# Reordering weight combinations and rebuilding the last drain in a Fourier-filter and SiLU-layer kernel

## The chip, the core and the metric

The kernel runs on one core of a Trainium2 chip. The metric is the device time of one execution in microseconds. The engines are called by the names of the profile: PE (TensorE), PEld (TensorE's weight loads), DVE (VectorE), ACT (ScalarE), POOL (GpSimd) and SP (SyncE, which here only issues DMAs). A name with a q, such as SPq, is the queue in which that engine issues DMAs or waits.

## What is computed

A Fourier filter over the sequence, then a two-matrix layer with a SiLU between. The weights come as 64-bit floats, everything else as 32-bit floats.

```python
X = np.fft.rfft(x, axis=1)                       # x: (8, 3008, 256)
Y = X * (filt_r + 1j * filt_i)[None, :, :]
y = np.fft.irfft(Y, n=x.shape[1], axis=1)
h = y.reshape(24064, 256) @ w_in                 # w_in: (256, 2048), 64-bit
g = h * (1.0 / (1.0 + np.exp(-h)))
out = g @ w_out                                  # w_out: (2048, 256), 64-bit
```

## The kernel before

The filter of each of the 8 sequences is done with small matrix multiplications in four stages (pa or pf, pb, pc, pd in the profile, with intermediate results written to DRAM and read back), and leaves the sequence in an SBUF tile y. The layer works on pieces of 256 or 240 tokens of two half-sequences at once, called pairs: 6 pairs a sequence, 48 in all. For each pair the 2048 inner columns are taken in 8 blocks of 256; one block of one pair is a step, so there are 384 steps, and one more in which only the last projection is left. Both matrix products use a Strassen-Winograd scheme, seven block products in place of eight. For that the weights need, beside their four blocks A11, A12, S3 and A22, three combinations, and S3 itself is replaced: `combine_weights` (line 853) computes in its part 0 S1 = S3 + A22 and S2 = S1 - A11, and in its part 1 S3 = A11 - S3 and S4 = A12 - S2.

A step has 8 rounds. In them `hidden(step)` (line 639) issues the seven products with the first matrix into the PSUM tiles px and pyz, their evictions and sums (abc and g) on ACT and DVE, and the SiLUs on ACT; `project(step - 1)` (line 698) issues the seven products of the step before with the second matrix into four PSUM accumulators acc. The two are interleaved round by round, so that one step's matmuls cover the other's work on DVE and ACT. The tiles px and pyz have one buffer each: TensorE can start the next product into one of them only when what was there has been read. In what follows, S4, S3, A11 and so on also name the matmul that uses this block; g0, g1 and g2 are the sums that `hidden` writes to g[:, 0], g[:, 1] and g[:, 2] (lines 663, 682 and 674).

Everything else is a list of pieces with a step and a round each: `put(step, round, piece)` (line 559), and similar entries for tokens and stores at the end of the program. The list is sorted by time, and after each round the pieces that are due are issued behind that round's work (`until`, line 1023). The order of the program on each engine is exactly this order; no scheduler changes it, and each engine works through its instructions in order.

Of these pieces the following matter here:

- The weights are rounded from 64 to 32 bits on the chip, 128 inner columns at a time (index j, 0 to 15; block jp = j // 2 of the weights needs both of its j). Weights 0 to 8 are done before the main loop. Weights 9 to 15 come in steps 0 to 6: `split` in round 1 (lines 812 to 816, on DVE and ACT), `rounded` (lines 828 to 834, on DVE), `placed` in round 5 (line 843, two DVE operations that write w_t). When j is odd the block is complete, and its combinations follow: part 0 in round 5 of the same step, part 1 in round 5 of the next one, and for j = 15 in the same one (lines 1001 to 1003). A combination is one DVE operation of 128 x 256, at line 623, the line of the helper `combine`.
- `tokens(pair)` (line 629) prepares three combinations of a pair's tokens on DVE; for pair 1 in step 7, round 1 (line 1015).
- Steps 0 to 7 also hold the first filter stage of the second sequence (`stage1`, line 325: two matmuls pa, two evictions on ACT, and DMAs by POOL at line 349).
- `drain(pair, i)` (line 719) is called when accumulator i of a pair is complete, in the order 0 to 3. It copies the accumulators to an SBUF tile s, alternately on ACT and DVE (lines 729 and 731), and then makes seven sums in s: on POOL, and for the last pair on DVE.
- `output(pair, chunk)` (line 736) transposes two of the four results of a pair (line 741) and issues eight stores of 28 or 32 KB (line 749), all by SP, and for the last pair by SP and ACT in turn. Chunk 0 needs outputs 2 and 6 of s, chunk 1 outputs 4 and 1.

Of the kernel before, what the change touches and what calls it, by code (L numbers as in the profile page):

```python
# [49 lines left out]
ALU = mybir.AluOpType  # L50
# [117 lines left out]
def kernel(  # L168
# [9 lines left out]
    nc = tc.nc  # L178
# [380 lines left out]
    def put(step, rnd, piece, *args):  # L559

        pending.append((step + rnd / ROUNDS, len(pending), lambda: piece(*args)))
# [55 lines left out]
    pairs = [(b, half, c0, n) for b in range(B) for half in range(2) for c0, n in PAIRS]  # L617
    n_steps = len(pairs) * NJP
    v, gp = nc.vector, nc.gpsimd
    ty, g_t, acc, unfinished = {}, {}, {}, []  # L620

    def combine(eng, out, in0, in1, op):
        eng.tensor_tensor(out=out, in0=in0, in1=in1, op=op)  # L623
# [5 lines left out]
    def tokens(pair):  # L629

        n, yt = pairs[pair][3], channels(pair)
        t = typool.tile([128, 4, CH], FP32, name=f"ty_{pair}", tag="ty")
        combine(v, t[:, 0:2, 0:n], yt[:, :, n:2 * n],
                yt[:, 0, 0:2 * n].rearrange("p (a n) -> p a n", a=2), ALU.subtract)
        combine(v, t[:, 2, 0:n], yt[:, 1, n:2 * n], t[:, 0, 0:n], ALU.subtract)
        combine(v, t[:, 3, 0:n], yt[:, 1, 0:n], t[:, 2, 0:n], ALU.subtract)
        ty[pair] = t
# [60 lines left out]
    def project(step):  # L698

        pair, jp = divmod(step, NJP)  # L700
        n, g = pairs[pair][3], g_t.pop(step)
        if jp == 0:
            acc[pair] = {}
        last = jp == NJP - 1

        order = PROJECT[2:3] + PROJECT[0:2] + PROJECT[3:] if jp == 0 else PROJECT
        for c, k, i, h in order:
            if i not in acc[pair]:
                acc[pair][i] = accps.tile([128, 2, 256], FP32, name=f"acc_{pair}_{i}", tag=f"a{i}")

            nc.tensor.matmul(out=acc[pair][i][:, h, 0:n], lhsT=w_t[:, jp, c, 1], rhs=g[:, k, 0:n],  # L711
                             start=(jp == 0 and h == 0), stop=last, skip_group_check=True)
            if last and (h == 1 or i == 3):
                drain(pair, i)
            yield
# [3 lines left out]
    def drain(pair, i):  # L719
        n = pairs[pair][3]  # L720

        if i == 0:
            results[pair] = spool.tile([128, 8, CH], FP32, name=f"s_{pair}", tag="s")
            if n < CH:
                gp.memset(results[pair][:, :, n:CH], 0.0)
        s = results[pair]
        copy = v.tensor_copy if i % 2 else nc.scalar.copy
        if i < 3:
            copy(out=s[:, 2 * i:2 * i + 2, 0:n], in_=acc[pair][i][:, :, 0:n])  # L729
            return  # L730
        copy(out=s[:, 6, 0:n], in_=acc.pop(pair)[3][:, 0, 0:n])
        eng = v if pair == len(pairs) - 1 else gp
        for o, a, b in ((2, 0, 2), (5, 0, 5), (3, 5, 3), (6, 3, 6), (0, 5, 1), (4, 0, 4), (1, 3, 1)):
            combine(eng, s[:, o, 0:n], s[:, a, 0:n], s[:, b, 0:n], ALU.add)

    def output(pair, chunk):

        b, half, c0, n = pairs[pair]
        o = opool.tile([128, 8, 2, 32], FP32, name=f"o_{pair}_{chunk}", tag="o")
        for h in range(2):  # L740
            v.transpose(out=o[:, :, h, :], in_=results[pair][:, ((2, 6), (4, 1))[chunk][h], :])
        row = (c0 + n * chunk) // 16
        for rr in range(2):
            cnt = (n // 16 - rr + 1) // 2
            t0 = b * S + 32 * (row + rr) + 16 * half
            for q in range(4):
                p0 = 32 * q + 16 * rr
                queue = nc.scalar if pair == len(pairs) - 1 and q % 2 else nc.sync
                queue.dma_start(
                    out=bass.AP(tensor=out.tensor, offset=out.offset + t0 * C + 64 * q,  # L750
                                ap=[[C, 16], [64 * C, cnt], [1, 64]]),
                    in_=o[p0:p0 + 16, 0:cnt].rearrange("p k h c -> p k (h c)"))
# [118 lines left out]
    def split(*js):  # L871
        if wide:
            split_weights(*js)

    def rounded(*js):
        if wide:
            round_weights(*js)
# [120 lines left out]
    for j in range(9, NJ):  # L998
        put(j - 9, 1, lambda j=j: (split(j), rounded(j)))
        put(j - 9, 5, placed, j)  # L1000
        if j % 2:
            put(j - 9, 5, combine_weights, j // 2, 0)
            put(j - 8 if j < 15 else j - 9, 5, combine_weights, j // 2, 1)

        if j < 11:
            put(j - 9, 1, weights, j + 5)

    per = len(PAIRS) * 2


    combines = ((-2, 1), (6, 1), (11, 5), (22, 5), (26, 6), (38, 1))
    stores = (((10, 1), (10, 5)), ((19, 1), (23, 5)), ((31, 1), (31, 5)), ((35, 1), (35, 5)),
              ((43, 1), (43, 5)), ((50, 1), (51, 1)))
    for pair in range(len(pairs)):
        step, rnd = combines[pair % per] if pair != 1 else (7, 1)
        pending.append((pair // per * STEPS + step + rnd / ROUNDS, 98, lambda pair=pair: tokens(pair)))
        for chunk in range(2):
            step, rnd = stores[pair % per][chunk]
            pending.append((pair // per * STEPS + step + rnd / ROUNDS, 99 + chunk,
                            lambda pair=pair, chunk=chunk: output(pair, chunk)))  # L1020
# [49 lines left out]
```

## Time and profile before

| | us |
|---|---|
| median of 4 runs | 2599.91 |
| lowest and highest of them | 2596.86, 2602.36 |
| the profiled execution, its own time | 2600.09 |
| its span in the trace | 2598.3 |
| PE busy in the span | 2566.3 |
| DVE busy | 1695.1 |
| ACT busy | 1105.4 |
| POOL busy | 423.9 |

The span runs from the first to the last event in the trace; the execution's own time has 1.8 us around it. The granted TensorE clock is 0.995 over the span. In the trace one matmul of the program stands as two, so "x2" in a line of PE is one product. A line of the timeline gives start, duration, engine, source line, operation, what is written and read, the number of instructions that were merged, and in brackets the idle time before it with the event that ended it. A merged line's duration runs from the start of its first instruction to the end of its last.

The first matmul of the main loop starts at 83.56 us; the last accumulation matmul ends at about 2587.5.

### The profile page before, as it was taken

What the parts mean: (1) busy time and instruction counts of PE and PEld (TensorE: products, weight loads), DVE (VectorE), ACT (ScalarE), POOL (GpSimd) and SP (SyncE); (2) the same over time, 40 slices, a digit from 0 to 9 for tenths busy, and PEclk for the clock granted to TensorE, in tenths of its full rate; (3) what the DMA queues carried; (4) which work ended last, traced back from release to release, by engine and by line L of the source; (5) the groups of instructions that cost most, each with busy time, mean ns of one, the idle gap of its engine ahead of it and who ended that gap; (6) DMA issues with size and microseconds to landing.
All of it is one profiled execution on the core that took longest, in us unless ns stands there. A gap on an engine that the chain in (4) does not pass through costs nothing.

```text
span 2598.3 us, 48343 instructions
## 1 busy us (share of the span) xinstructions
PE 2566.3 (99%) x18928; PEld 2186.9 (84%) x18928; DVE 1695.1 (65%) x3574; ACT 1105.4 (43%) x3015; POOL 423.9 (16%) x667
## 2 busy tenths in 40 slices
PE   8899999999999999999999999999999999999998
PEld 6688888888888888888888888888888888888987
DVE  7766666666666766666666676666666676555554
ACT  3544444444444444443444444444444444444443
POOL 2111211121112111311122111211121112101100
PEclk9899999999999999999999999999999999999999
DMA  8531232212222222222223222331223211201000
GB/s 273 143 89 45 68 78 65 66 56 79 62 57 66 76 65 56 62 78 67 62 64 77 62 66 57 73 81 50 63 71 75 72 41 26 60 18 21 9 17 16
DMA packets 200253, 171.08 MB, mean 66 GB/s; under 512 B 122324, under 2 KB 174388, under 8 KB 199236
## 3 DMA queue, kind: packets, MB, share of 16 engines
q1 hardware_dynamic: 178616, 117.07, 18.6%
q0 software_dynamic: 16864, 44.59, 5.5%
q10 hardware_dynamic: 4544, 6.33, 0.8%
q8 instruction: 149, 2.44, 0.4%
q14 instruction: 80, 0.66, 0.1%
HBM read 96.05 MB, written 81.26 MB: 68 GB/s over the span
## 4 chain that ended last, share of the span: by engine, by line
PE 97%; DMA 2%; DVE 1%; ACT 0%; ACTq 0%; issue 0%; SPq 0%; DVEq 0%
PE acc L711 44%; PE px L652 26%; PE pyz L652 19%; PE pd L538 3%; PE pb L433 2%; PE pc L469 2%; PE pf L403 1%; PE pa L331 0%; PE pa L340 0%; DMA filt<-in_filt_i_dram 0%; PE pc L491 0%; DMA w_t<-in_x_dram 0%; DMA t<-d 0%; DMA raw<-in_moe_w_in_dram 0%; DMA filt<-in_filt_r_dram 0%
## 5 line engine op out<-in xcount | busy, mean ns | idle before, releaser
L711 PE MATMUL acc<-g,w_t 128*128 128x256 f32 (+1 forms) x5376 | 1512.1, 375 | 0.4 <-DVE g L623 0.4
L711 PEld LDWEIGHTS acc<-g,w_t 128*128 128x128 f32 x5376 | 1021.4, 190 | 115.6 <-DVE g L623 0.8
L623 DVE TENSOR_TENSOR g<-pyz,abc 128x256 f32<-128x256 f32 (+1 forms) x1152 | 479.6, 416 | 538.1 <-ACT abc L673 297.2
L623 DVE TENSOR_TENSOR g<-g 128x256 f32<-128x256 f32 (+3 forms) x1152 | 616.8, 535 | 196.7 <-ACT g L656 183.5
L652 PE MATMUL px<-ty,w_t 128*128 128x256 f32 (+1 forms) x2304 | 686.8, 380 | 0.5 <-ACT abc L673 0.5
L656 ACT ACTIVATE g<-g 128x256 f32<-128x256 f32 (+1 forms) x1152 | 472.9, 411 | 245.8 <-DVE g L623 245.8
L623 POOL TENSOR_TENSOR s<-s 128x256 f32<-128x256 f32 (+1 forms) x329 | 259.8, 807 | 1454.4 <-DVE s L729 1438.1
L652 PEld LDWEIGHTS px<-ty,w_t 128*128 128x128 f32 x2304 | 424.0, 190 | 82.9 <-issue 25.9
L652 PE MATMUL pyz<-y,w_t 128*128 128x256 f32 (+1 forms) x1536 | 453.7, 377 | 0.7 <-DVE g L623 0.6
L652 PEld LDWEIGHTS pyz<-y,w_t 128*128 128x128 f32 x1536 | 283.4, 189 | 46.6 <-DVE g L623 5.8
L667 ACT COPY abc<-px 128x256 f32<-128x256 f32 (+1 forms) x384 | 141.3, 368 | 364.9 <-PE px L652 364.9
L656 ACT ACTIVATE g<-px 128x256 f32<-128x256 f32 (+1 forms) x384 | 145.8, 380 | 307.5 <-PE px L652 307.5
L673 ACT COPY abc<-px 128x256 f32<-128x256 f32 (+1 forms) x384 | 143.8, 374 | 309.9 <-PE px L652 309.9
L652 PE MATMUL px<-y,w_t 128*128 128x256 f32 (+1 forms) x768 | 229.6, 381 | 0.9 <-ACT y L246 0.9
L652 PE MATMUL pyz<-ty,w_t 128*128 128x256 f32 (+1 forms) x768 | 225.6, 375 | 0.0
L652 PEld LDWEIGHTS px<-y,w_t 128*128 128x128 f32 x768 | 141.9, 189 | 39.9 <-ACT g L656 15.4
L652 PEld LDWEIGHTS pyz<-ty,w_t 128*128 128x128 f32 x768 | 146.0, 190 | 16.9 <-DVE g L623 0.5
L660 ACT COPY abc<-px 128x256 f32<-128x256 f32 (+1 forms) x384 | 134.9, 351 | 2.5 <-PE px L652 1.1
L244 DVE COPY y<-pd 128x376 f32<-128x376 f32 x62 | 50.0, 806 | 102.1 <-PE pd L538 102.0
L538 PEld LDWEIGHTS pd<-wi_t,t 48*64 48x64 f32 x4096 | 67.5, 138 | 28.9 <-issue 28.9
L246 ACT COPY y<-pd 128x376 f32<-128x376 f32 x62 | 50.2, 809 | 87.2 <-PE pd L538 87.0
L538 PE MATMUL pd<-wi_t,t 48*64 48x47 f32 x4096 | 75.2, 237 | 9.3 <-DMA t<-d 9.0
(98 smaller groups left out, 1323.3 us busy)
## 6 DMA issues: line engine op xcount, KB each, us to landing
t<-d SPq DMA_DIRECT2D x120, 192.0 KB
d<-q POOLq DMA_DIRECT2D x86, 256.0 KB, 2.7
t<-d SPq DMA_DIRECT2D x84, 256.0 KB
out_dram<-o SPq DMA_DIRECT2D x636, 32.0 KB
d<-tf POOLq DMA_DIRECT2D x144, 96.0 KB, 2.4
xr<-in_x_dram SPq DMA_DIRECT2D x6, 1472.0 KB
x_all<-in_x_dram SPq DMA_DIRECT2D x72, 96.0 KB
x_all<-xr SPq DMA_DIRECT2D x72, 96.0 KB
```

What stands on the lines that cost most here:

```text
L244: nc.vector.tensor_copy(out=dst, in_=src)
L246: nc.scalar.copy(out=dst, in_=src)
L433: nc.tensor.matmul(out=ps[k][32 * j:32 * j + 32, ri, :], lhsT=d_t[rows, 4 * g + at, ri, :], rhs=t2[rows, at, :], start=True, stop=True)
L469: nc.tensor.matmul(out=ps[j][64 * k:64 * k + 64, a, :], lhsT=e_t[rows, g + a, k, ri, :], rhs=zs[k][rows, ri, :], start=(a == 0 and ri == 0 ...
L538: nc.tensor.matmul(out=ps[h][c0:c0 + 64, cb, i, :], lhsT=t4s[g][rows, i, 128 * cb + c0:128 * cb + c0 + 64], rhs=wi_t[rows, :], start=True, ...
L623: eng.tensor_tensor(out=out, in0=in0, in1=in1, op=op)
L652: nc.tensor.matmul(out=out, lhsT=w_t[:, jp, c, 0], rhs=rhs, start=start, stop=True, skip_group_check=True)
L656: nc.scalar.activation(out=g[:, k, 0:n], in_=g[:, k, 0:n] if src is None else src, func=AFT.Silu)
L660: nc.scalar.copy(out=sums[:, 0, 0:n], in_=xo)
L667: nc.scalar.copy(out=sums[:, 1, 0:n], in_=xo)
L673: nc.scalar.copy(out=sums[:, 2, 0:n], in_=xo)
L711: nc.tensor.matmul(out=acc[pair][i][:, h, 0:n], lhsT=w_t[:, jp, c, 1], rhs=g[:, k, 0:n], start=(jp == 0 and h == 0), stop=last, skip_group ...
```

## The change

There are three parts. First, the combinations of weights 9, 11, 13 and 15 move: part 0 from the step of the rounding to the next one (for 15 to round 6 of the same step), and part 1 one step further than part 0 (for 13 to step 6, round 1; for 15 to step 7, round 1). In the order of DVE this puts part 0 of 9, 11 and 13 ahead of line 843's operations of weights 10, 12 and 14, part 1 of 9 and 11 ahead of those of weights 11 and 13, part 1 of 13 ahead of the split of weight 15, and takes two of the four combinations behind weight 15's placement to the next step. Pair 1's tokens go from round 1 to round 5 of step 7.

Second, the last pair's drain doesn't copy all accumulators: a new function copies the first one and half of the third on ACT, and the sums take the other operands straight from PSUM, on DVE. Outputs 2 and 6 are computed first, chunk 0 is transposed and its stores are issued, and only then follow the three sums of chunk 1. Two copies on DVE fall away; the number of sums stays seven.

Third, the last pair's stores: chunk 0's eight are issued by SP (three), ACT (three) and POOL (two), chunk 1's by SP and ACT (four each).

The instructions of PE and their order stay as they are.

```diff
@@ drain
         s = results[pair]
+        if pair == len(pairs) - 1:
+            return drain_last(pair, i, n, s, acc[pair])
         copy = v.tensor_copy if i % 2 else nc.scalar.copy
...
-        eng = v if pair == len(pairs) - 1 else gp
         for o, a, b in ((2, 0, 2), (5, 0, 5), (3, 5, 3), (6, 3, 6), (0, 5, 1), (4, 0, 4), (1, 3, 1)):
-            combine(eng, s[:, o, 0:n], s[:, a, 0:n], s[:, b, 0:n], ALU.add)
+            combine(gp, s[:, o, 0:n], s[:, a, 0:n], s[:, b, 0:n], ALU.add)
+
+    def drain_last(pair, i, n, s, sums):
+
+        def add(o, a, b):
+            combine(v, s[:, o, 0:n], s[:, a, 0:n], b, ALU.add)
+        if i == 0:
+            nc.scalar.copy(out=s[:, 0:2, 0:n], in_=sums[0][:, :, 0:n])
+        elif i == 1:
+            add(2, 0, sums[1][:, 0, 0:n])
+        elif i == 2:
+            add(5, 0, sums[2][:, 1, 0:n])
+            nc.scalar.copy(out=s[:, 4, 0:n], in_=sums[2][:, 0, 0:n])
+            add(3, 5, sums[1][:, 1, 0:n])
+        else:
+            add(6, 3, sums[3][:, 0, 0:n])
+            output(pair, 0)
+            for o, a, b in ((0, 5, 1), (4, 0, 4), (1, 3, 1)):
+                add(o, a, s[:, b, 0:n])
+            output(pair, 1)
@@ output
-                queue = nc.scalar if pair == len(pairs) - 1 and q % 2 else nc.sync
+                queue = nc.sync
+                if pair == len(pairs) - 1:
+                    turn = (0, 1, rr, 2) if chunk == 0 else (0, 1, 0, 1)
+                    queue = (nc.sync, nc.scalar, nc.gpsimd)[turn[q]]
@@ for j in range(9, NJ)
         if j % 2:
-            put(j - 9, 5, combine_weights, j // 2, 0)
-            put(j - 8 if j < 15 else j - 9, 5, combine_weights, j // 2, 1)
+
+            put(*((j - 8, 5) if j < 15 else (j - 9, 6)), combine_weights, j // 2, 0)
+            put(*((j - 7, 5) if j < 13 else (j - 7 if j == 13 else j - 8, 1)), combine_weights, j // 2, 1)
@@ for pair in range(len(pairs))
-        step, rnd = combines[pair % per] if pair != 1 else (7, 1)
+        step, rnd = combines[pair % per] if pair != 1 else (7, 5)
...
-        for chunk in range(2):
+        for chunk in range(2 if pair < len(pairs) - 1 else 0):
```

## Prediction

> **What bounds the kernel now.** I read the page first, then two stretches that the diff touches: the first eight steps of the main loop and the end.
>
> ```profile
> span 2598.3 us, 48343 instructions
> PE 2566.3 (99%) x18928; PEld 2186.9 (84%) x18928; DVE 1695.1 (65%) x3574; ACT 1105.4 (43%) x3015; POOL 423.9 (16%) x667
> PE 97%; DMA 2%; DVE 1%; ACT 0%; ACTq 0%; issue 0%; SPq 0%; DVEq 0%
> ```
>
> TensorE is busy in 99% of the span and is 97% of the chain that ended last. No matmul is added or removed, so only its idle time can be won: 2598.3 - 2566.3 = 32 us, most of it before the main loop, which the diff doesn't touch. The stretch table (us, length, then busy time and instructions of PE, PEld, DVE, ACT, POOL, clock, DMA share, GB/s), cut at the first matmul of each step, gives what lies in steps 1, 2, 6, 7 and 8:
>
> ```profile
> 91.10:99.43 8.33, 8.26 (x34) 6.01 (x34) 6.72 (x17) 4.65 (x12) 2.23 (x5) 1.00 0.47 145
> 99.43:107.28 7.85, 7.85 (x33) 5.93 (x32) 6.24 (x16) 4.41 (x12) 1.97 (x5) 1.00 0.71 210
> ...
> 131.33:139.18 7.85, 7.85 (x34) 5.94 (x33) 6.24 (x16) 4.42 (x12) 1.97 (x5) 1.00 0.69 164
> 139.18:147.83 8.65, 8.03 (x34) 5.99 (x33) 5.22 (x13) 3.50 (x10) 2.04 (x6) 1.00 0.19 46
> 147.83:153.87 6.04, 6.04 (x29) 5.29 (x28) 3.46 (x8) 3.34 (x10) 0.79 (x2) 1.00 0.65 178
> ```
>
> Step 8 is pure matmul work: 6.04 us. Steps 1 to 7 also have two stage-1 matmuls, 1.72 us in the chain, so their work is 7.76. They take 8.33, 7.85, 8.10, 7.85, 8.10, 7.85, 8.65 (steps 3 to 5 are in the same table): 2.41 us over the work. In the timeline (start, us, engine, line, operation, [idle before it and its releaser]) the end of step 0 and of step 6:
>
> ```profile
> 90.25 0.75 DVE L843 TENSOR_TENSOR w_t<-m,e 128x256 f32<-128x256 f32 x2
> 91.03 0.88 DVE L623 TENSOR_TENSOR w_t<-w_t 128x256 f32<-128x256 f32 x2
> 91.84 0.42 DVE L623 TENSOR_TENSOR g<-pyz,abc 128x256 f32<-128x256 f32 x1
> ...
> 138.88 1.55 DVE L623 TENSOR_TENSOR w_t<-w_t 128x256 f32<-128x256 f32 x4
> 140.35 0.41 DVE L623 TENSOR_TENSOR g<-pyz,abc 128x256 f32<-128x256 f32 x1
> 140.82 0.70 PE L652 MATMUL pyz<-y,w_t 128*128 128x256 f32 x2 [0.62 <-DVE g L623]
> ```
>
> VectorE places rounded weights (L843), combines them (w_t<-w_t), and only then reads pyz (g<-pyz); TensorE's next step waits for that read. At the end:
>
> ```profile
> 2585.61 1.89 PE L711 MATMUL acc<-g,w_t 128*128 128x240 f32 x8 [0.41 <-DVE g L623]
> 2586.37 0.56 ACT L729 COPY s<-acc 128x480 f32<-128x480 f32 x1 [1.51 <-PE acc L711]
> ...
> 2587.86 2.68 DVE L623 TENSOR_TENSOR s<-s 128x240 f32<-128x240 f32 x7
> 2590.46 1.42 DVE L741 STREAM_TRANSPOSE o<-s 128x256 f32<-128x256 f32 x4
> 2591.25 3.77 SPq L749 DMA_DIRECT2D out_dram<-o  x8
> 2591.25 3.97 ACTq L749 DMA_DIRECT2D out_dram<-o  x8
> ```
>
> After TensorE's last matmul (2587.5): 3.7 us of copies, seven sums and two transposes until the first store, 4.0 us of issuing, then about 3.1 us of landing and closing.
>
> [...] The trace has 402 for s<-s. [...] the trace has 0.41 us for g<-pyz at 240 beside 0.40 for s<-s, so I take nothing[...]. [...] here issuing (0.36 to 0.49 us a store) sets the pace. [...] POOL's four issues from 97.99 take 1.97 us (498 ns each) beside VectorE's w_t work.
>
> **Weights, part by part.** VectorE, ScalarE and TensorE form a loop through each step: g1 (g<-pyz) -> silu -> three g operations -> split L812 -> ScalarE L814, L816, L667, silu, two evictions, L673 -> g2 -> weight work -> g1. Its length sets steps 1 to 6. By the starts of g1 it is 7.85 us in odd steps (91.84 to 99.69; weight work: part-1 combinations, two independent operations, ahead of L843, 98.35 to 99.69 = 1.34), and 8.10 in even ones (99.69 to 107.79; L843, then part-0 combinations that need it and each other, 106.20 to 107.79 = 1.59). So: independent order 0.67 + 0.67; waiting for L843 0.11 more; the dependent pair 0.14 more.
> - Step 0: part 0 leaves. g1 is then held by its matmul (S4 ends about 91.15): 91.18 instead of 91.84, gain 0.66. In step 1 the stage-1 matmuls come only 0.34 earlier, since TensorE won only that; the second eviction waits for them, and L673 comes 0.52 earlier. Gain 0.52.
> - Steps 1, 3, 5: part 0 ahead of L843 instead of part 1: +0.14 each. Steps 2, 4: part 1 ahead of L843 instead of part 0 behind it: -0.25 each. Gain after step 5: 0.52 - 0.42 + 0.50 = 0.60.
> - Step 6: part 1 of weight 13 goes into round 1, ahead of split(15). Behind it on VectorE stand L812 and L815, and ScalarE's L814, L816, then L667 wait for those: +0.67, so TensorE stalls again at S3 and A22. Part 1 of weight 15 leaves the end of the step: -0.66. Net nothing: g1 about 139.75 instead of 140.35, TensorE's pyz 140.22 instead of 140.82.
> - Step 7: part 1 of weight 15 (0.67) takes the tokens' place in round 1; TensorE reads S3 only at about 144. Tokens (1.5 us) move to round 5, between g2 and g1: g1 about 147.57, where its matmul alone would give 147.43. Cost 0 to 0.14. Nothing needs the tokens before step 8, round 2. From step 8 VectorE has 2.6 us free a step.
> Sum: **-0.55 us** (bounds: -0.1 if step 6 and 7 cost their full price at TensorE; -3.1 if all 2.41 and step 0's 0.66 went).
>
> **The end, part by part.** The first copy on ScalarE ends 2586.93. Pitches from the seven s<-s: 0.42 for an add that needs the one before, 0.33 otherwise (3 x 0.42 + 3 x 0.33 = 2.25 from first to last start; measured 2.26).
> - Sums of outputs 2, 5, 3, 6 from 2586.96: starts 2586.96, 2587.29, 2587.71, 2588.13. The last accumulator is ready at 2587.51, so no add waits for TensorE. VectorE's two copies (0.66 + 0.41) go. [...]
> - Four semaphore checks, 0.1 us apart, stand ahead of each chunk's first transpose (2589.83 to 2590.12 in the trace of before, under two adds). Behind one add they show about 0.1. Transposes 2588.58, 2588.94; chunk 0 stores from **2589.35** (before 2591.25).
> - Three adds 2589.27, 2589.69, 2590.02, transposes to 2591.10: chunk 1 ready 2591.12.
> - Chunk 0 has three stores on SP, three on ACT, two on POOL; the HW queues issue theirs by 2590.8. Chunk 1: four each from 2591.12, last starts about 2592.45 (SP) and 2592.5 (ACT), against 2594.58 and 2594.78. A store also waits until the earlier store with its semaphore has landed: before, chunk 1 started at 2593.21 and 2593.45, 1.96 and 2.20 after those of chunk 0. Now the first of chunk 1 take free ones and the second ones come 2.1 to 2.2 after theirs: at most 0.1.
> - POOL: two stores of 0.50 to 0.54 us (L349, L517), issued by 2590.45, landing 2.4 to 2.9 later (medians of the DMA table): 2593.4. ACT's last lands about 2592.5 + 2.2 = 2594.7. Covered by 1.3 us. Nothing is queued behind POOL's two stores or ScalarE's waiting copy but ACT's own stores, which wait for VectorE anyway.
> - Packets: 2176 in 4.3 us before, at best 240 in 0.35 us, so 3.2 us at that rate; the new stretch is about 4 us.
> Sum: 2594.78 - 2592.55 = **-2.2 us** (bounds [...] -2.4 without the 0.1s).
>
> Total -2.75: 2600.09 (the profiled execution, span 2598.3 and 1.8 around it) becomes 2597.3. The median of the four is 2599.91, so **2597.2**.
>
> **Rivals.**
> 1. Weights give nothing: step 6's delay is not paid back because ScalarE's chain ends last there. For it: L667 and L673 are the releasers in the chain of step 6. Only the end: -2.2, 2597.7.
> 2. The end is bound by landing: 16 stores from three queues share the 16 DMA engines, which were 0.6 to 0.8 busy. If landing rises from 2.2 to 2.9, chunk 1's stores wait for chunk 0's: last at 2590.3 + 2.9 = 2593.2, -1.5; total -2.05, 2597.9.
> 3. More than the sum: all idle time of steps 0 to 7 goes, -3.1 and -2.4: 2594.4. Against it: the loop of 7.85 is longer than the work.
> 4. Slower: POOL's queue ends last. Its landings reached 18.3 us (L517) and 6.7 (L349) at most, beside other traffic. It decides from 2594.7 on; the kernel is slower once the second store lands over 2597.4, 7.5 us after its issue at 2589.9. At 18.3 it lands 2608.2, 10.7 us later: 2610. Against it: the queues are empty then.
>
> **Chances.** Forecast 0.62; rival 1 0.14; rival 2 0.10; rival 3 0.10; rival 4 0.04. Runs of one kernel spread from 2596.86 to 2602.36, so a median of a few lies some 1.5 us off either way: 2594.4 to 2599.8. About 0.2% (5.2 us) is what a measurement can tell from no change. Faster than 2594.7 needs rival 3 or luck: 0.12. Slower than 2605.1 is rival 4: 0.04. Within: 0.84.
>
> **What would show it.** Step 0's end without w_t<-w_t and pyz at about 92.07; step 6 with w_t<-w_t before L812 and a wait of TensorE for L667 or L673; step 8's first matmul about 0.55 us earlier; at the end the first store issued 1.8 us after the last matmul's end (before 3.7), the last one 5.0 after it (before 7.3), and POOL's two landed before ACT's last. Wrong if the first steps differ by over 1 us either way, if a DMA of POOL's ends last, or if TensorE waits anywhere after step 8 that it didn't before.

## The result, and the profile after

| | before | after |
|---|---|---|
| median, us | 2600.09 (61 runs) | 2596.74 (41 runs) |
| lowest and highest | 2596.86, 2602.81 | 2594.43, 2600.70 |
| the profiled execution | 2600.09 | 2596.69 |
| its span | 2598.3 | 2594.9 |

The ratio is 0.9989, with an interval of 0.9984 to 0.9993 (the quotient of the two medians, 0.9987, lies inside it): a little faster, by 1.8 to 4.2 us, which is less than the 0.2% that the prediction called no change. The forecast was 2597.2.

The page of the changed kernel says that TensorE does the same work in a span that is 3.4 us shorter; VectorE has two instructions fewer (the two copies), POOL two more (its two stores):

```profile
span 2594.9 us, 48346 instructions
...
PE 2565.2 (99%) x18928; PEld 2186.5 (84%) x18928; DVE 1694.2 (65%) x3572; ACT 1105.2 (43%) x3015; POOL 425.0 (16%) x669
```

The stretch table of the changed kernel, cut at the first matmul of steps 1, 2, 6, 7 and 8, in the columns of the prediction:

```profile
90.90:98.76 7.86, 7.86 (x33) 6.17 (x33) 6.14 (x15) 4.66 (x12) 2.32 (x6) 1.00 0.49 159
98.76:106.66 7.90, 7.90 (x34) 5.91 (x33) 6.33 (x17) 4.42 (x12) 1.90 (x4) 1.00 0.69 210
...
130.34:138.98 8.64, 8.38 (x33) 5.83 (x32) 7.04 (x18) 4.41 (x12) 1.96 (x5) 1.00 0.62 146
138.98:146.96 7.98, 7.98 (x33) 5.99 (x32) 4.79 (x12) 3.50 (x10) 2.05 (x6) 1.00 0.21 50
146.96:153.08 6.12, 6.12 (x29) 5.21 (x28) 3.79 (x9) 3.35 (x10) 0.79 (x2) 1.00 0.65 174
```

Step 1 is down from 8.33 to 7.86, and step 7 from 8.65 to 7.98. But step 6, of 7.85 before, is now the long one, with 8.64: the length that step 7 lost stands there. In the timeline of the changed kernel, the end of step 0 and then step 6:

```profile
90.04 0.75 DVE L866 TENSOR_TENSOR w_t<-m,e 128x256 f32<-128x256 f32 x2
90.98 0.42 DVE L623 TENSOR_TENSOR g<-pyz,abc 128x256 f32<-128x256 f32 x1 [0.19 <-PE pyz L652]
91.86 0.59 PE L652 MATMUL pyz<-y,w_t 128*128 128x256 f32 x2
...
133.35 0.75 DVE L623 TENSOR_TENSOR w_t<-w_t 128x256 f32<-128x256 f32 x2
...
135.63 0.35 ACT L667 COPY abc<-px 128x256 f32<-128x256 f32 x1
136.03 0.70 PE L652 MATMUL px<-ty,w_t 128*128 128x256 f32 x2 [0.26 <-ACT abc L667]
...
139.96 0.70 PE L652 MATMUL pyz<-y,w_t 128*128 128x256 f32 x2
```

In step 0 no combination stands any more between the placement (L866, before L843) and the read of pyz, and VectorE now waits for TensorE there (0.19) instead of the other way round. In step 6 two combinations of weight 13 stand ahead of the split (L835, next on VectorE at 134.03); behind them ACT's copy L667 comes late, and TensorE waits 0.26 for it.

The end of the changed kernel, in the timeline:

```profile
2584.87 1.89 PE L711 MATMUL acc<-g,w_t 128*128 128x240 f32 x8 [0.41 <-DVE g L623]
2585.64 0.56 ACT L742 COPY s<-acc 128x480 f32<-128x480 f32 x1 [1.51 <-PE acc L711]
2586.23 1.67 DVE L623 TENSOR_TENSOR s<-s,acc 128x240 f32<-128x240 f32 x4 [0.53 <-ACT s L742]
...
2587.92 0.77 DVE L761 STREAM_TRANSPOSE o<-s 128x256 f32<-128x256 f32 x2
...
2588.72 3.55 SPq L772 DMA_DIRECT2D out_dram<-o  x7
2588.72 3.69 ACTq L772 DMA_DIRECT2D out_dram<-o  x7
2588.99 1.12 POOL L772 DMA_DIRECT2D out_dram<-o  x2 [28.58 <-DVE s L623]
```

Four sums straight from PSUM instead of copies and seven sums; then the first transposes, and the stores start 3.85 us after the start of TensorE's last group of accumulations. Before they started 5.64 after it (2591.25 - 2585.61).

Where the 3.4 us of the span lie, by the starts of steps and groups in the two traces:

| stretch | before | after | change |
|---|---|---|---|
| start to the loop's first matmul | 83.56 | 83.35 | -0.21 |
| from there to step 1 | 7.54 | 7.55 | +0.01 |
| step 1 to step 9 | 62.77 | 62.18 | -0.59 |
| step 9 to TensorE's last group | 2431.74 | 2431.79 | +0.05 |
| last group to the end of the span | 12.69 | 10.03 | -2.66 |

Spans are given to 0.1 us, so the last row and all ends below are good to about 0.05 us. The first row lies ahead of everything that the change moves; the experiments show that it varies by more than this from run to run.

### The profile page after: what moved, and what is told of

It reads as the page before. It is cut to its first block, busy times and chain, and to the rows that moved or that the text cites. A ratio compares the mean times of both kernels' runs of the same rounds, so it can differ in the third digit from the quotient of the medians.

```text
span 2594.9 us, 48346 instructions
## 1 busy us (share of the span) xinstructions
PE 2565.2 (99%) x18928; PEld 2186.5 (84%) x18928; DVE 1694.2 (65%) x3572; ACT 1105.2 (43%) x3015; POOL 425.0 (16%) x669
## 4 chain that ended last, share of the span: by engine, by line
PE 95%; DMA 2%; DVE 1%; ACT 1%; issue 0%; POOL 0%; SPq 0%; ACTq 0%; DVEq 0%; POOLq 0%
PE acc L711 43%; PE px L652 26%; PE pyz L652 19%; PE pd L538 3%; PE pb L433 2%; PE pc L469 2%; PE pf L403 1%; DMA filt<-in_filt_r_dram 1%; PE pa L340 0%; DMA w_t<-in_x_dram 0%; DVE g L623 0%; PE pc L491 0%; DMA t<-d 0%; ACT t L344 0%; DVE w_t L623 0%
## 5 line engine op out<-in xcount | busy, mean ns | idle before, releaser
L667 ACT COPY abc<-px 128x256 f32<-128x256 f32 (+1 forms) x384 | 141.3, 368 | 364.9 <-PE px L652 364.9
```

The costliest lines, as they stand in the source:

```text
L667: nc.scalar.copy(out=sums[:, 1, 0:n], in_=xo)
```

## The experiments

The theory is the prediction's: the combinations act through the loop of VectorE and ScalarE in steps 0 to 8, and the end is a chain of sums, transposes, issuing and landing. Its four rivals, by number: the weights give nothing; stores from three queues land later; all the idle time of the first steps goes; POOL's queue ends last. All stage times below are from traces: step lengths from first matmul to first matmul, times at the end from the start of TensorE's last group of accumulations. e5, e7, e8 and e10 to e12 were executed once each, so only their traces are used.

### The halves alone

e1_only_weights is the kernel before with the new places of the combinations and of pair 1's tokens:

```diff
-            put(j - 9, 5, combine_weights, j // 2, 0)
-            put(j - 8 if j < 15 else j - 9, 5, combine_weights, j // 2, 1)
+            put(*((j - 8, 5) if j < 15 else (j - 9, 6)), combine_weights, j // 2, 0)
+            put(*((j - 7, 5) if j < 13 else (j - 7 if j == 13 else j - 8, 1)), combine_weights, j // 2, 1)
...
-        step, rnd = combines[pair % per] if pair != 1 else (7, 1)
+        step, rnd = combines[pair % per] if pair != 1 else (7, 5)
```

> The combinations and pair 1's tokens are moved as in the change; the last pair's drain and stores are as before. If VectorE and ScalarE set the pace of steps 0 to 6, the steps' starts counted from the loop's first matmul are those of the changed kernel: step 8 starts about 63.6 us after it instead of 64.3 before, with the long step now step 6 (8.6 us) and not step 7. If the 0.6 us came from elsewhere (the time before the loop, chance in the weights' loads), step 8 starts 64.2 to 64.4 after it. From the start of the last accumulation group to the end of the span: 12.7 us as before, under either. The time: 0.5 us less, which the runs can hardly tell from nothing (ratio 0.9998).

e2_only_end is the changed kernel with these three lines as before, so only with the new drain and the new queues.

> The drain and the stores of the last pair are as in the change, the combinations and the tokens as before. Step 8 starts 64.3 us after the loop's first matmul as before. From the start of the last accumulation group to the end of the span: 10.0 us if the 2.7 us lie in the end alone; more if the shorter landing in the changed kernel was chance (up to 10.6). The time: 2.2 to 2.7 us less than before, ratio about 0.9990.

| | step 1 to 8 | step 1 to 9 | last store starts | end | ratio to before, interval |
|---|---|---|---|---|---|
| before | 56.73 | 62.77 | 9.17 | 12.69 | |
| after | 56.06 | 62.18 | 7.10 | 10.03 | 0.9989, 0.9984 to 0.9993 |
| e1_only_weights | 56.07 | 62.19 | 9.24 | 12.83 | 1.0003, 0.9995 to 1.0012 |
| e2_only_end | 56.72 | 62.76 | 7.03 | 10.12 | 0.9989, 0.9982 to 0.9995 |

The two halves don't touch each other: e1 has the steps of the changed kernel and the end of the one before, e2 the reverse. e1's steps 6 and 7 in the stretch table, to within 0.01 of the changed kernel's:

```profile
131.33:139.98 8.65, 8.39 (x34) 5.83 (x32) 7.04 (x18) 4.42 (x12) 1.97 (x5) 1.00 0.61 156
139.98:147.96 7.98, 7.98 (x33) 5.99 (x32) 4.79 (x12) 3.49 (x10) 2.04 (x6) 1.00 0.21 50
```

Rival 1 falls: without the new end the weights still win 0.58 from step 1 to step 9. The times of e1 can't show it: their interval reaches from 1.3 us faster to 3.1 us slower. One reason is seen in its trace: the loop began at 84.60 us, 1.04 later than in the trace of before, and nothing of the change comes ahead of it. Whether that happened in its other executions too isn't shown. The expectations of step 8's start, counted from the loop's first matmul, were missed for a like reason (63.36 us in e1 in place of 63.6, 63.26 in e2 in place of 64.3): step 0 took 7.29 us in e1 and 6.55 in e2, where it took 7.54 before. Over the profiled executions of all these kernels the loop begins between 83.3 and 86.8 us, and step 0 takes 6.5 to 8.3; step 1 begins between 90.4 and 95.1, a scatter wider than the whole gain of the change. So the weights' part can be read from step 1 on in a trace, and not from these times.

### Queues and order at the end

e3_no_pool takes POOL out; chunk 0 goes to SP and ACT, four stores each:

```diff
-                    turn = (0, 1, rr, 2) if chunk == 0 else (0, 1, 0, 1)
+                    turn = (0, 1, 0, 1)
```

> The changed kernel, but chunk 0's eight stores go to SP and ACT, four each; POOL issues none. Now all eight completion semaphores are taken by chunk 0, and each store of chunk 1 waits until one of chunk 0 has landed. The last store starts about 7.45 us after the start of the last accumulation group (7.10 with POOL). If POOL's two stores shortened the landing, because they take packets off the other two queues, the end comes 3.5 us after that start, in all 10.9; if the landing is short because the two chunks' stores lie apart, it comes 2.9 after it, in all 10.4.

e4_only_queues is the kernel before, its drain kept, with the changed kernel's queues:

```diff
-                queue = nc.scalar if pair == len(pairs) - 1 and q % 2 else nc.sync
+                queue = nc.sync
+                if pair == len(pairs) - 1:
+                    turn = (0, 1, rr, 2) if chunk == 0 else (0, 1, 0, 1)
+                    queue = (nc.sync, nc.scalar, nc.gpsimd)[turn[q]]
```

> The kernel before with one thing changed: chunk 0's eight stores are issued by SP (three), ACT (three) and POOL (two). The sums are as before, so the first store starts 5.6 us after the start of the last accumulation group. With three stores a queue chunk 1's first start about 0.65 us earlier, its second and later ones wait for landings: last start 8.4 to 8.7 (9.17 before). If POOL's stores shorten the landing too, the end is at 11.4 to 11.7; if not, at 11.9 to 12.2 (12.7 before).

| | last store starts | end | from one to the other | stores by SP, ACT, POOL |
|---|---|---|---|---|
| before | 9.17 | 12.69 | 3.52 | 8, 8, 0 |
| e4_only_queues | 8.83 | 11.72 | 2.89 | 7, 7, 2 |
| e3_no_pool | 7.46 | 10.95 | 3.49 | 8, 8, 0 |
| after | 7.10 | 10.03 | 2.93 | 7, 7, 2 |

The new order of the sums alone (before to e3) is worth 1.74; POOL's two stores are worth 0.92 behind it (e3 to after) and 0.97 on the old drain (before to e4), so the two add up. The parts are the same both times: 0.34 to 0.36 because the last store starts earlier, as predicted for one pitch of a queue, and 0.56 to 0.63 that nobody predicted, behind the last start (taken apart below). e4's last start missed its expectation by 0.1. In times, e3 is at 0.9992 (0.9984 to 1.0001), e4 at 0.9998 (0.9989 to 1.0006): an end shorter by 0.97 is not resolved.

### The combinations in VectorE's own wait

The waits of the changed kernel in steps 0 to 7 (engine, tile and line that wait, what for, us in total, times, longest) hold a place where VectorE has nothing to do. L851 is the first operation of `rounded`, which waits for ScalarE's part of the split:

```profile
DVE m L851 <- ACT m L839: 6.8, 7, 1.0
```

That is 1.0 us in each of seven steps, as before the change (there L828 for L816, with the same three numbers), and a pair of combinations takes 0.75. e5_gap13 puts only part 1 of weight 13 there, the one that made step 6 long:

```diff
-        put(j - 9, 1, lambda j=j: (split(j), rounded(j)))
+        between = [lambda: combine_weights(6, 1)] if j == 15 else []
+        put(j - 9, 1, lambda j=j, between=between: (split(j), [f() for f in between], rounded(j)))
...
-            put(*((j - 7, 5) if j < 13 else (j - 7 if j == 13 else j - 8, 1)), combine_weights, j // 2, 1)
+            if j != 13:
+                put(*((j - 7, 5) if j < 13 else (j - 8, 1)), combine_weights, j // 2, 1)
```

> The changed kernel, but part 1 of weight 13 stands in step 6 between the split and the rounding of weight 15, where VectorE waits 1 us for ScalarE anyway, and no longer ahead of the split. If its 0.67 us ahead of the split is what lengthens step 6 to 8.6 us (ScalarE's queue waits for L812, TensorE for ScalarE), step 6 takes 7.9 to 8.0 and step 8 starts 55.3 to 55.5 us after step 1 (56.06 in the changed kernel, 56.73 before). If step 6 is long for another reason (the evictions, the stage-1 matmuls), nothing moves: 56.0 to 56.1.

Step 6 fell from 8.64 to 7.97, and the stretch from step 1 to step 8 from 56.06 to 55.40: the 0.67 of two combinations. So it was their place ahead of the split that made step 6 long.

e6_gap_all puts both parts of weights 9, 11 and 13 into that wait in steps 1 to 6, and leaves weight 15 as in the changed kernel:

```diff
-        put(j - 9, 1, lambda j=j: (split(j), rounded(j)))
+        k = j - 10
+        between = [lambda k=k: combine_weights(4 + k // 2, k % 2)] if k >= 0 else []
+        put(j - 9, 1, lambda j=j, between=between: (split(j), [f() for f in between], rounded(j)))
...
-            put(*((j - 8, 5) if j < 15 else (j - 9, 6)), combine_weights, j // 2, 0)
-            put(*((j - 7, 5) if j < 13 else (j - 7 if j == 13 else j - 8, 1)), combine_weights, j // 2, 1)
+            if j == 15:
+                put(j - 9, 6, combine_weights, 7, 0)
+                put(j - 8, 1, combine_weights, 7, 1)
```

> The changed kernel, but the parts 0 and 1 of weights 9, 11 and 13 stand in round 1 of steps 1 to 6, each between the split and the rounding of that step's weight, in VectorE's wait for ScalarE. If the loop of VectorE and ScalarE sets the pace of these steps, it is now 7.2 us and shorter than TensorE's work: steps 2 to 6 take 7.76 to 7.85 each and step 8 starts 54.6 to 54.9 us after step 1 (56.06 in the changed kernel). If something else sets it, 55.3 (the gain of step 6 alone) or 56.1. The time: 1.2 to 1.5 us less than the changed kernel, 0.9983 to 0.9984 of before.

Its stretch table for steps 2, 6 and 8, and the same line of its waits:

```profile
101.70:109.50 7.80, 7.80 (x34) 5.98 (x32) 6.37 (x15) 4.41 (x12) 1.89 (x4) 1.00 0.66 206
132.90:140.70 7.80, 7.80 (x34) 5.98 (x32) 6.66 (x16) 4.41 (x12) 1.97 (x5) 1.00 0.61 174
148.68:154.80 6.12, 6.12 (x29) 5.21 (x28) 3.80 (x9) 3.35 (x10) 0.78 (x2) 1.00 0.63 169
```

```profile
DVE m L851 <- ACT m L839: 2.4, 7, 1.0
```

VectorE's wait went from 6.8 to 2.4 us, steps 2 to 6 all take 7.80, and TensorE is busy through the whole of each. Step 1 to 8 takes 54.85, 1.21 less than in the changed kernel. The time is at 0.9979 (0.9970 to 0.9989) of before.

In e6 step 8 still has 6.12 where 6.04 is pure work. e9_gap_tokens moves pair 1's tokens of e6 from (7, 5) to (7, 2):

```diff
-        step, rnd = combines[pair % per] if pair != 1 else (7, 5)
+        step, rnd = combines[pair % per] if pair != 1 else (7, 2)
```

> The kernel of e6 (parts 0 and 1 of weights 9, 11 and 13 in VectorE's wait for ScalarE), and pair 1's tokens in round 2 of step 7, behind part 1 of weight 15, where VectorE has 2.6 us free. If the tokens between g2 and g1 are what makes step 8 take 6.12 in place of 6.04, it takes 6.04 now, and step 9 starts 60.9 us after step 1 (60.97 in e6, 62.18 in the changed kernel, 62.77 before). If not, 60.97. The end as in the changed kernel, 10.0 us. The time: 1.2 to 1.3 us below the changed kernel, ratio to before 0.9984.

```profile
146.21:152.25 6.04, 6.04 (x30) 5.29 (x28) 3.46 (x8) 3.34 (x10) 0.78 (x2) 1.00 0.65 181
```

Step 8 is back at 6.04, and step 1 to 9 takes 60.89, 1.29 less than in the changed kernel. The time is 2596.17 over 20 runs, at 0.9982 (0.9976 to 0.9989) of before. This is the best version in the traces from step 1 on; in the times it can't be told from the changed kernel, whose interval overlaps.

### What lies behind the last store

e7_left_out is the changed kernel without POOL's two stores (60 KB of the last pair's output are not written):

```diff
+                    if turn[q] == 2:
+                        continue
```

> The changed kernel without the two stores of chunk 0 that POOL issues: 60 KB of the last pair's output are not written; SP and ACT issue the same fourteen. If POOL's stores shorten the end because SP's and ACT's queues have fourteen stores in place of sixteen, the end is 9.7 to 10.0 us after the start of the last accumulation group (10.03 with POOL, 10.95 with sixteen). If it is something in POOL's queue itself, 10.4 to 10.6.

e8_pool_twice gives POOL two stores of chunk 1 as well:

```diff
-                    turn = (0, 1, rr, 2) if chunk == 0 else (0, 1, 0, 1)
+                    turn = (0, 1, rr, 2)
```

> The changed kernel with POOL taking two stores of chunk 1 as well. SP's and ACT's last stores start about 0.4 us earlier. POOL starts its own 0.27 us after the others and takes 0.56 for each, so they land about 2.5 us after 6.5, at 9.0, as the last ones of SP and ACT do: the end at 9.6 to 10.1 us after the start of the last accumulation group. If a store of POOL can be as late as 6.7 us after its issue, as the slowest of its first stage were, 13 or more.

e10_one_pool leaves POOL one store:

```diff
-                    turn = (0, 1, rr, 2) if chunk == 0 else (0, 1, 0, 1)
+                    turn = (0, 1, 0, 2 if rr == 0 else 1) if chunk == 0 else (0, 1, 0, 1)
```

> The changed kernel with one store of chunk 0 on POOL in place of two; ACT takes the other, so SP and ACT have fifteen. POOL's drain, which ended 9.1 us after the start of the last accumulation group, ends 0.56 earlier, at 8.6, and can't be last. If each store more on SP's and ACT's queues lengthens the last landing, the end is between the one of fourteen (10.0) and of sixteen (10.95): about 10.5, of which 0.2 to 0.35 is ACT's later last store. If only POOL's drain sets the end of the changed kernel, the end is at 9.5 to 9.8.

e11_last_left_out is e3 without the last two stores of chunk 1, which are not written (about 56 KB):

```diff
+                    if chunk == 1 and rr == 1 and q > 1:
+                        continue
```

> The kernel of e3 (no stores by POOL) without the last two stores of chunk 1, one of SP and one of ACT: some 56 KB of the output are not written. Fourteen stores on the two queues as in e7, but chunk 0 keeps eight, and so all semaphores are in use when chunk 1 comes. The last store then starts 6.95 to 7.0 us after the start of the last accumulation group. If the number of stores on the two queues makes the last landing long (3.5 from the last start to the end with sixteen, 2.9 to 3.1 with fourteen), the end is at 9.9 to 10.1; if it is the reuse of the semaphores by chunk 1, at 10.4 to 10.5.

e12_eight_on_sp keeps POOL's two stores and gives SP eight, ACT six:

```diff
-                    turn = (0, 1, rr, 2) if chunk == 0 else (0, 1, 0, 1)
+                    turn = (0, 1, 0, 2) if chunk == 0 else (0, 1, 0, 1)
```

> The changed kernel with chunk 0's stores dealt four to SP, two to ACT, two to POOL; with chunk 1's, SP has eight stores, ACT six, fourteen in all on the two. So far the end came 3.4 to 3.6 us after the last store's start where SP, or SP and ACT, had eight stores (sixteen or fifteen in all), and 2.8 to 3.2 where each had seven. SP's last store starts about 7.3 to 7.4 us after the start of the last accumulation group. If an eighth store on one queue makes the last landing long, the end is at 10.7 to 10.9; if the sum over the two queues does, at 10.2 to 10.4.

| | stores by SP, ACT, POOL | last store of SP or ACT starts | end | from one to the other |
|---|---|---|---|---|
| after | 7, 7, 2 | 7.10 | 10.03 | 2.93 |
| e7_left_out | 7, 7, 0 | 7.03 | 10.11 | 3.08 |
| e11_last_left_out | 7, 7, 0 | 6.93 | 9.81 | 2.88 |
| e12_eight_on_sp | 8, 6, 2 | 7.70 | 10.42 | 2.72 |
| e10_one_pool | 8, 7, 1 | 7.40 | 10.81 | 3.41 |
| e3_no_pool | 8, 8, 0 | 7.46 | 10.95 | 3.49 |
| e8_pool_twice | 6, 6, 4 | 6.64 | 11.86 | 5.22 |

(In e10 it was SP that got the extra store, and not ACT, as the expectation said.) Leave e8 aside for a moment. With fourteen stores on SP and ACT together the end comes 2.7 to 3.2 us behind the last start, with fifteen or sixteen 3.4 to 3.6; before, e1, e2, e4, e5, e6 and e9 (3.52, 3.59, 3.09, 2.89, 2.96, 2.97 and 3.16) fall on the same sides. It isn't POOL's doing: e7 and e11 have no store by POOL. It isn't that one queue has eight: e12. Two expectations were missed here: e12's last start (7.70, expected 7.3 to 7.4), although its gap was the shortest of all, and e10's end (10.81, expected about 10.5). e7 and e11 came within about 0.1 of the ends expected for fourteen stores.

The traces themselves tell where the half microsecond lies. Before and after the change, each store of the last pair names a semaphore there, a counter that is raised 16 times as the store lands and that the queues wait for. SP's and ACT's stores have eight of them; the first eight stores take one each, and the later ones use them again (before the change, SP's second store with number 105 starts at 2593.21, 0.06 us behind the last update by its first, at 2593.15). At the program's end SP checks these eight one after another, in every trace in the same order: 101, 103, 104, 105, 106, 107, 108, 110, by the numbers that the trace gives. In the traces with fifteen or sixteen stores (before, e1, e3, e10) the last to land has number 101, which SP checks first, and the other seven checks come behind it. With fourteen it has 108 (110 in e12), and one check or none is left. SP's checks from the last landing on, first before, then after the change (number, ns shortest, median and longest, first and last start):

```profile
L1065 SPq EVENT_SEMAPHORE  x8: 28/28/28, 2596.6 to 2597.4; - x8
```

```profile
L1089 SPq EVENT_SEMAPHORE  x2: 28/28/28, 2594.0 to 2594.0; - x2
```

Eight checks, or two. So the stretch behind the last start falls into three parts:

| | last start to last landing | place of its check | landing to the last check's end | from there to the end |
|---|---|---|---|---|
| before | 1.80 | 1 of 8 | 0.83 | 0.86 |
| e3_no_pool | 1.83 | 1 of 8 | 0.83 | 0.87 |
| e10_one_pool | 1.71 | 1 of 8 | 0.85 | 0.87 |
| after | 1.97 | 7 of 8 | 0.11 | 0.87 |
| e7_left_out | 2.08 | 7 of 8 | 0.10 | 0.88 |
| e11_last_left_out | 1.77 | 7 of 8 | 0.20 | 0.88 |
| e12_eight_on_sp | 1.77 | 8 of 8 | 0.04 | 0.87 |

The landing doesn't get shorter with fewer stores (1.77 to 2.08 with fourteen, 1.71 to 1.83 with fifteen or sixteen), and the closing is the same (0.86 to 0.88); the gain lies in the checks. Of the 0.83 some 0.33 is one pause between two of them, for which no cause is seen. No run changes the order of the checks alone.

e8 is another matter. Each of its four stores by POOL landed in 2.3 to 2.6 us, yet the end came 1.8 later than the latest that was expected with such landings (10.1). In the groups of the program's last line, first of e8, then of the changed kernel (number, then ns shortest, median and longest, and the first and last start):

```profile
L1089 SPq DRAIN  x3: 7/7/7, 2596.3 to 2598.0; - x3
L1089 POOLq DRAIN  x3: 40/102/4711, 2593.0 to 2598.2; - x3
```

```profile
L1089 POOLq DRAIN  x3: 40/102/4613, 2589.4 to 2594.7; - x3
```

In e8 POOL closes its queue with one instruction, a DRAIN of 4.7 us. It starts at 2593.0 and ends at 2597.7, 1.4 after SP was through with its own waits for landing (2596.3); what is left of the span, 0.8, is common closing. In the changed kernel the same instruction runs from 2589.4 to 2594.0, while SP finishes at 2594.1: nearly a tie. In the kernels whose POOL issues no store at the end (before, e1, e3, e7 and e11) it takes 3.9 us and is over some 30 us ahead of the end, at 2564.8 before the change. POOL's last store starts 1.80 later in e8 than in the changed kernel, and the end comes 1.83 later.

## Why the prediction was right, step by step

**What bounds the kernel.** TensorE's work didn't change (2566.3 and 2565.2 busy), and from step 9 to the last group it took 2431.74 and 2431.79. So the change added no time there that can be seen (0.05).

**The weights.** The reader of pyz in one step stands beside the first matmuls of the next, so what the prediction says of step n is seen in the length of step n + 1:

| what | predicted | measured, in | |
|---|---|---|---|
| part 0 leaves step 0 | -0.52 | -0.47 | step 1 |
| steps 1 and 3: part 0 ahead of the placement | +0.14 each | +0.05, +0.12 | steps 2, 4 |
| steps 2 and 4: part 1 ahead of it | -0.25 each | -0.25, -0.24 | steps 3, 5 |
| steps 5 and 6: +0.14; weight 13 ahead of the split, paid back by weight 15's leaving | +0.14 | +0.12 (+0.79, -0.67) | steps 6, 7 |
| tokens | 0 to 0.14 | +0.08 | step 8 |
| sum | -0.55 | -0.59 | |

The two that were expected to cost 0.14 alike took 0.05 and 0.12; why they differ isn't shown. The trace also has TensorE's first matmul into pyz behind step 0's read of it at 91.86, which is the predicted 92.07 less the 0.21 by which this execution's loop began earlier. Rival 1's mechanism is real, TensorE does wait for L667 in step 6 (0.26), but it is paid back in step 7; e5 shows that it need not be paid at all. Rival 3 didn't come, and e6 and e9 show why: most of the idle time was not to be had by moving work to the next step, in front of the same readers. It took moving it into VectorE's wait.

**The end.** Predicted -2.2, measured -2.66. By terms:

- First store at 3.74 (2589.35 - 2585.61), measured 3.85. Most of the 0.1 lies in the sums: four take 1.67 where three pitches and one add give 1.58, the fourth being 0.09 late behind a semaphore wait in VectorE's queue (at 2587.43). The reads from PSUM take no longer, as the prediction had it: these four sums take 397 to 405 ns each, the seven from SBUF before took 398 to 408. ACT's copy for output 4 waited 0.79 us for a sum of VectorE and ended at 2587.34, 1.7 us ahead of the sum that reads it.
- Last store at 6.9, measured 7.10. Here is rival 2 in small: one store of ACT's second chunk started at 6.73 where the others' pitch puts it near 6.5, held until the earlier store with its semaphore had landed, at 6.71. Otherwise rival 2 falls: the slowest landing of SP's and ACT's stores rose from 2.24 to 2.45 us and not to 2.9, and e3 without the third queue ends 0.92 later.
- Landing and closing after the last start were taken as unchanged, 3.5 us. They took 2.93. **This is the term that was mis-sized**: -0.59, the largest error in the sum. The prediction took as one piece what the traces show as three: the last landing (1.80, now 1.97), SP's checks behind it (0.83, now 0.11) and the common closing (0.86 and 0.87). That the third queue would save issue time and nothing more was the author's estimate. The measurements agree as far as the transfers go: the issue time is there, 0.34 to 0.36, and the last landing takes no less. The rest comes from this program's closing: with two stores fewer on the eight semaphores, the last to land has one that SP checks near the end of its list (seventh of eight, before first). The prediction had no reason to expect it; this part of the gain was luck.
- POOL's two stores: starts at 4.12 and 4.67 and issues of 0.56 us against the predicted 0.50 to 0.54, landing after 2.4 and 2.6. But **that they are covered by 1.3 us was wrong**. That counted their landing; what ends last on POOL is the closing of its queue, and its cover is about 0.1 us. Rival 4 was thus nearer than its 4 in 100: not by a late landing, which was the reason it gave, but by this instruction. And e8, with POOL's last store 1.80 later, lost 1.83 of the 2.66 that the change won at the end (11.86 against 10.03; before 12.69).

**The sum.** -0.55 and -2.2 became -0.59 and -2.66; with -0.21 ahead of the loop and +0.06 elsewhere this is the 3.4 of the profiled executions, and the medians differ by as much. That these agree to 0.1 is partly luck: with loops that begin at 83.3 to 86.8 us, the time of one execution says little about 0.6 us. The mechanism of the weights and the order of the end were right; without the 0.59 of the closing the end would have won 2.07, close to the predicted 2.2.

## What to carry to other kernels

Work that must be done on an engine beside the critical loop belongs into a wait of that same engine, not merely into a later step: the 1.0 us that VectorE stood idle between `split` and `rounded` in every step was in the waits all along, and took the combinations for nothing, where moving them one step on won a third as much (0.67 against 1.88 us from step 1 to step 8). At the end of a kernel, count every queue to its closing, not to its landing: POOL's DRAIN (4.3 to 4.7 us here, where its stores land in 2.3 to 2.6), and the completion checks that still stand behind the last landing (0.83 us before, 0.11 after). And where a part of a change is smaller than what varies ahead of it, measure it between two marks in the trace and not by the time.

## What the runs showed of the hardware

- POOL's queue ended with a DRAIN of 4.3 to 4.7 us in every kernel in which it issued stores at the end (4340 ns in e10, 4502 in e12, 4613 after, 4711 in e8), although the stores land in 2.3 to 2.6. In the kernels without such stores it took 3.9.
- SP's eight completion checks took 0.83 to 0.85 us behind the last landing where that landing was the first to be checked (before, e1, e3, e10), and 0.04 where it was the last (e12). The last store of SP or ACT landed 1.7 to 2.1 us after its start, with fourteen stores on the two queues as with sixteen.
- A sum with one operand in PSUM (128x240, 32-bit) took VectorE as long as one with both in SBUF: 397 to 405 ns in the changed kernel, 398 to 408 before.
